# Transposes of attention operands: from TensorE and VectorE copies to DMA transposes on the SP queue

## Chip, cores, metric

One core of a Trainium2 chip. The metric is the device time of one execution in microseconds, all runs in the fast state unless said.

## The reference, cut

Attention over keys and values that are averaged in groups of 8, for 8 batches, 8 heads, 576 rows, head size 64; then a mixture of 4 two-layer networks on the 4608 x 512 result.

```python
k_p = k.reshape(B, H, Sp, pool, D).mean(axis=3)          # Sp = 72
v_p = v.reshape(B, H, Sp, pool, D).mean(axis=3)
scores = scale * np.matmul(q, k_p.transpose(0, 1, 3, 2))
attn = softmax(scores)                                    # exp, sum, division
x = (attn @ v_p) -> (4608, 512)
for e in range(4):
    h = np.maximum(x @ w1[e], 0.0)                        # 512 -> 1024
    out += p[:, e:e + 1] * (h @ w2[e])                    # 1024 -> 512
```

## The kernel before

The matmuls of the networks (`up`, `down`) run in chunks of 512 rows, one for each batch (chunk c takes the first 512 rows of batch c) and a ninth for the 64 remainder rows of each batch. While chunk c runs, the attention of batch c + 1 is cut into pieces that are slipped in between its groups of eight matmuls. A chunk has 32 slots for pieces, one after each `up` or `down` group. Attention needs four kinds of transposes: the keys (`kpT`), the queries (`qT`, `qTr` for the remainder rows), and the attention's result (`xT`, `x_rem`). Before, each is a group of TensorE transposes into PSUM and a copy out of it:

```python
def keys(b, hs):
    kpt_ps = psum_a.tile([P, H, SP], BF16, tag="a", name="kpt_ps")
    for h in range(hs.start, hs.stop):
        nc.tensor.transpose(kpt_ps[:, h, :], state[("kp", b)][:, h], ident[:SP, :SP])
    nc.vector.tensor_copy(out=state[("kpT", b)][:, hs], in_=kpt_ps[:, hs])

def queries(b, pair):                       # 4 pairs of heads a batch
    qt_ps = pool.tile([P, 2, 2, P], BF16, tag=tag, name="qt_ps")
    ...  # 4 transposes of q_sb, then one copy to qT

def flip(x_tok, dst, copy=nc.vector.tensor_copy):   # turn(b, r), rem_turn(i)
    xt_ps = psum_a.tile([P, NPAIR, P], BF16, tag="a", name="xt_ps")
    for kc in range(KC):
        nc.tensor.transpose(xt_ps[:, kc, :], flat[:, kc * P:(kc + 1) * P], ident[:])
    copy(out=dst, in_=xt_ps[:])

# main loop (cut)
per_slot = len(pieces) / (SLOTS - 2 - late)         # late = 16 in chunk 0, else 0
for i in range(NR):
    up(c, e, ...)
    slot()                                          # pops the pieces that are due
    down(*steps[s - 1], i)
    slot()
```

The softmax here doesn't subtract the row's maximum and nothing guards it: scores larger than these inputs give would overflow.

Of the kernel before, what the change touches and what calls it, by code (L numbers as in the profile page):

```python
# [12 lines left out]
BF16 = mybir.dt.bfloat16  # L13
# [4 lines left out]
def kernel(  # L18
# [10 lines left out]
    nc = tc.nc  # L29

    B, H, S, D = q.shape
    E, DM, F = moe_w1.shape
    P = nc.NUM_PARTITIONS
    NPAIR = H // 2
    POOL = 8
    SP = S // POOL
    NT = 512
    NR = NT // P
    REM = S - NT
    KC = DM // P  # L40
# [6 lines left out]
    const = ctx.enter_context(tc.tile_pool(name="const", bufs=1))  # L47
# [14 lines left out]
    w2_bf = wpool.tile([P, E, FCH, DM], BF16, name="w2_bf")  # L62
    x_rem = const.tile([P, NPAIR, NT], BF16, name="x_rem")
    ident = const.tile([P, P], BF16, name="ident")
    vps = [const.tile([SP, H, D + 1], BF16, name=f"vp{i}") for i in range(3)]

    raws = {}
# [33 lines left out]
    def load_k(b):  # L101
        load_kv(b, k, "kraw")
# [49 lines left out]
    def fold_keys(b, hs):  # L152
        raw = raws[("kraw", b)]
        fold(raw, hs)
        if hs.start == 0:
            state[("kp", b)] = apool.tile([SP, H, 2, D], BF16, name="kp")

        for dup in range(2):
            nc.vector.tensor_add(out=state[("kp", b)][:, hs, dup, :], in0=raw[:, hs, 0, :],  # L159
                                 in1=raw[:, hs, 1, :])  # L160

    def keys(b, hs):
        if hs.start == 0:
            state[("kpT", b)] = apool.tile([P, H, SP], BF16, name="kpT")
        kpt_ps = psum_a.tile([P, H, SP], BF16, tag="a", name="kpt_ps")
        for h in range(hs.start, hs.stop):
            nc.tensor.transpose(kpt_ps[:, h, :], state[("kp", b)][:, h], ident[:SP, :SP])  # L167
        nc.vector.tensor_copy(out=state[("kpT", b)][:, hs], in_=kpt_ps[:, hs])

    def fold_values(b, hs):  # L170
        raw = raws[("vraw", b)]
# [5 lines left out]
    def queries(b, pair):  # L177
        q_sb = raws[("q", b)]
        if pair == 0:
            state[("qT", b)] = apool.tile([P, H, 2, P], BF16, name="qT")  # L180
        pool, tag = (psum_o, "o_ps") if b == 0 else (psum_a, "a")
        qt_ps = pool.tile([P, 2, 2, P], BF16, tag=tag, name="qt_ps")
        for hh in range(2):
            for rr in range(2):
                nc.tensor.transpose(  # L185
                    qt_ps[:, hh, rr, :], q_sb[:, 2 * pair + hh, 2 * rr:2 * rr + 2, :], ident[:]
                )
        copy = nc.scalar.copy if b == 0 and pair % 2 else nc.vector.tensor_copy
        copy(out=state[("qT", b)][:, 2 * pair:2 * pair + 2], in_=qt_ps[:])  # L189

    def scores(b, pair):
        kpT, qT = state[("kpT", b)], state[("qT", b)]
        if pair == 0:
            state[("expT", b)] = apool.tile([SP, H, 2, 2, P], BF16, name="expT")
        expT = state[("expT", b)]
        both = [psum_a.tile([P, 2, 2, P], F32, tag="a", name="sc_ps") for _ in range(2)]
        for hh in range(2):
            h = 2 * pair + hh
            for r2 in range(2):
                lo = r2 * D  # L200
                nc.tensor.matmul(  # L201
                    both[r2][0:SP, hh], lhsT=kpT[lo:lo + D, h, :], rhs=qT[lo:lo + D, h]
                )
        for r2 in range(2):
            nc.scalar.activation(  # L205
                out=expT[:, 2 * pair:2 * pair + 2, :, r2, :], in_=both[r2][0:SP],
                func=ACT.Exp, scale=EXP_SCALE,
            )
# [19 lines left out]
            )  # L228
        divide(c_ps, state[("x", b, r)], half)

    def flip(x_tok, dst, copy=nc.vector.tensor_copy):
        xt_ps = psum_a.tile([P, NPAIR, P], BF16, tag="a", name="xt_ps")
        flat = x_tok[:].rearrange("p a h d -> p (a h d)")
        for kc in range(KC):
            nc.tensor.transpose(xt_ps[:, kc, :], flat[:, kc * P:(kc + 1) * P], ident[:])  # L235
        copy(out=dst, in_=xt_ps[:])  # L236

    def turn(b, r):
        if r == 0:
            state[("xT", b)] = xpool.tile([P, KC, NT], BF16, name="xT")  # L240
        flip(state.pop(("x", b, r)), state[("xT", b)][:, :, r * P:(r + 1) * P],
             nc.scalar.copy if b == 0 else nc.vector.tensor_copy)



    def rem_queries(i):
        q_rem = q_rems.pop(i)
        qt_ps = psum_a.tile([P, NPAIR, P], BF16, tag="a", name="qtr_ps")
        for pair in range(NPAIR):
            nc.tensor.transpose(  # L250
                qt_ps[:, pair, :], q_rem[:, 2 * pair:2 * pair + 2, :], ident[:]
            )
        qTr = apool.tile([P, NPAIR, 2, REM], BF16, name="qTr")
        nc.vector.tensor_copy(
            out=qTr[:].rearrange("p a b t -> p (a b t)"),
            in_=qt_ps[:].rearrange("p a t -> p (a t)"),
        )
        state[("qTr", i)] = qTr

    def rem_scores(i):  # L260
        qTr = state.pop(("qTr", i))
        both = [psum_a.tile([P, 2, NPAIR, REM], F32, tag="a", name="scr_ps") for _ in range(2)]
        for bb in range(2):
            kpT = state[("kpT", 2 * i + bb)]
            for pair in range(NPAIR):
                for hh in range(2):
                    lo = hh * D
                    nc.tensor.matmul(  # L268
                        both[hh][0:SP, bb, pair, :], lhsT=kpT[lo:lo + D, 2 * pair + hh, :],
                        rhs=qTr[lo:lo + D, pair, bb, :],  # L270
                    )
        expTr = apool.tile([SP, 2, 2, NPAIR, REM], BF16, name="expTr")
        for hh in range(2):
            nc.scalar.activation(out=expTr[:, hh], in_=both[hh][0:SP],
                                 func=ACT.Exp, scale=EXP_SCALE)
        state[("expTr", i)] = expTr
# [14 lines left out]
        state[("xr", i)] = x_tok  # L291

    def rem_turn(i):
        flip(state.pop(("xr", i)), x_rem[:, :, i * P:(i + 1) * P])

    def attention_first():

# [18 lines left out]
    def attention(b):  # L316

        every = slice(0, H)
        more = b + 1 < B
        pieces = []  # L320
        add = pieces.append

        def folded_keys():
            fold_keys(b, every)
            if more:
                load_k(b + 1)

        def folded_values():
            fold_values(b, every)
            if more:  # L330
                load_v(b + 1)

        def queried(pair):
            queries(b, pair)
            if more and pair == NPAIR - 1:
                load_q(b + 1)
                load_q_rem(b + 1)

        add(folded_keys)
        add(lambda: queried(0))  # L340
        add(folded_values)
        add(lambda: keys(b, every))
        for pair in range(1, NPAIR):
            add(lambda pair=pair: queried(pair))
            add(lambda pair=pair: scores(b, pair - 1))
        add(lambda: scores(b, NPAIR - 1))
        for r in range(NR):
            add(lambda r=r: (context(b, r, 0), context(b, r, 1)))
            if r:
                add(lambda r=r: turn(b, r - 1))  # L350
        add(lambda: turn(b, NR - 1))
        return pieces

    def attention_rem(i):
        return [lambda: rem_queries(i), lambda: rem_scores(i), lambda: rem_context(i),
                lambda: rem_turn(i)]



# [47 lines left out]

    for vp in vps:
        nc.vector.memset(vp[:, :, D:D + 1], float(POOL))
    make_identity(nc, ident[:])  # L410
    steps = [(c, e) for c in range(NCH) for e in range(E)]
    SLOTS = E * NR * 2


    ENG = mybir.EngineType
    with tc.manual_schedule(engines={ENG.PE, ENG.DVE, ENG.Activation, ENG.Pool}):
        load_k(0)
        load_q(0)
        load_v(0)
# [27 lines left out]
        for s in range(len(steps) + 1):  # L447
            if s < len(steps):
                c, e = steps[s]
                if e == 0:  # L450
                    while pieces:
                        pieces.popleft()()
                    if c % 2:
                        pieces.extend(attention_rem(c // 2))
                    if c + 1 < B:
                        pieces.extend(attention(c + 1))

                    late = SLOTS // 2 if c == 0 else 0
                    per_slot = len(pieces) / (SLOTS - 2 - late)
                    due = -late * per_slot  # L460
            for i in range(NR):
                if s < len(steps):
                    n = FCH // NR
                    up(c, e, range(i * n, (i + 1) * n))
                slot()
                if s > 0:
                    down(*steps[s - 1], i)
                slot()
# [30 lines left out]
```

## Time and profile before

| | before |
|---|---|
| time, median of 4 | 573.08 us (573.04 to 573.14) |
| span of the profiled run | 571.3 us |
| TensorE busy, granted clock | 96%, 0.998 |
| VectorE, ScalarE busy | 33%, 41% |
| first `up` matmul of chunk 1, of chunk 8 | 81.64 us, 503.4 us |

TensorE is the engine to read: its busy share is near all of the span. The prediction shows those lines (in a page, PE are TensorE's matmuls, PEld its weight loads, DVE is VectorE, ACT ScalarE, POOL GpSimd, SPq the DMA queue that SP fills; PEclk is the granted clock in tenths, DMA the busy share of the DMA engines in tenths). The DMA queues are wanted for a comparison later (packets, MB, share of 16 engines):

```profile
q0 software_dynamic: 31504, 22.63, 27.4%
q1 hardware_dynamic: 5248, 9.44, 4.9%
```

The first queue holds the loads, issued by GpSimd; the second the stores, issued by SP.

### The profile page before, as it was taken

How to read it: one execution, taken by the hardware profiler on the slowest of the kernel's cores; microseconds unless marked ns; L12 is line 12 of the kernel's file. 1: busy time of each engine (PE TensorE's matmuls, PEld its weight loads, DVE VectorE, ACT ScalarE, POOL GpSimd, SP SyncE). 2: the span in 40 equal slices, each digit the busy share in tenths (PEclk: the TensorE clock that was granted, in tenths of full speed). 3: DMA queues.
4: the chain of work that ended last, by engine and by line, in shares of the span. 5: the costliest groups of instructions: out<-in, count | busy, mean ns of one | idle time of the engine just before them, and what ended most of it. 6: DMA issues, size and time to landing. Idle time of an engine off the chain costs nothing.

```text
span 571.3 us, 7394 instructions
## 1 busy us (share of the span) xinstructions
PE 546.0 (96%) x3107; PEld 259.8 (45%) x3168; DVE 189.9 (33%) x397; ACT 235.2 (41%) x403; POOL 37.5 (7%) x52
## 2 busy tenths in 40 slices
PE   2699999999999999999999999999999999999996
PEld 1344454444444444444444444454445444444442
DVE  3504446134613335144414361346124211220122
ACT  2453534543354344533463335433543344334430
POOL 6410100010101001100110000100000000000000
PEclk9999999999999999999999999999999999999999
DMA  8999932530343005400730016301000010010003
GB/s 127 211 210 203 185 33 76 82 41 1 73 84 42 2 37 108 55 0 20 140 41 1 1 69 89 42 1 56 20 0 1 37 38 1 0 38 37 2 0 75
DMA packets 36787, 32.56 MB, mean 57 GB/s; under 512 B 8576, under 2 KB 30080, under 8 KB 36752
## 3 DMA queue, kind: packets, MB, share of 16 engines
q0 software_dynamic: 31504, 22.63, 27.4%
q1 hardware_dynamic: 5248, 9.44, 4.9%
q8 instruction: 25, 0.41, 0.3%
q14 instruction: 10, 0.08, 0.1%
HBM read 45.16 MB, written 9.44 MB: 96 GB/s over the span
## 4 chain that ended last, share of the span: by engine, by line
PE 90%; DMA 6%; DVE 1%; issue 1%; ACT 1%; POOL 0%; POOLq 0%
PE o_ps L381 42%; PE h_ps L371 41%; DMA q_sb<-in_q_dram 5%; PE sc_ps L201 2%; PE c_ps L226 1%; PE xt_ps L235 1%; PE qt_ps L185 1%; DMA kraw<-in_k_dram 1%; PE kpt_ps L167 0%; DVE x_tok L213 0%; ACT expT L205 0%; PE scr_ps L268 0%; PE c_ps L286 0%; PE qtr_ps L250 0%; POOL kraw L78 0%
## 5 line engine op out<-in xcount | busy, mean ns | idle before, releaser
L375 ACT ACTIVATE H_sb<-h_ps 128x512 bf16<-128x512 f32 x288 | 172.0, 597 | 255.4 <-PE h_ps L371 242.7
L381 PE MATMUL o_ps<-w_bf,H_sb 128*128 128x512 bf16 x1127 | 268.8, 379 | 1.7 <-issue 0.5
L371 PE MATMUL h_ps<-xT,w_bf 128*128 128x512 bf16 x991 | 240.8, 382 | 2.7 <-issue 0.7
L371 PEld LDWEIGHTS <-w_bf 128*128 128x128 bf16 x1152 | 109.4, 98 | 126.9 <-issue 7.9
L381 PEld LDWEIGHTS <-H_sb 128*128 128x128 bf16 x1152 | 108.8, 98 | 122.2 <-issue 1.4
L392 DVE SCALAR_TENSOR_TENSOR acc<-o_ps,p_all,acc 128x512 f32<-128x512 f32 x108 | 81.0, 750 | 214.6 <-PE o_ps L381 191.7
L389 ACT ACTIVATE acc<-o_ps,p_all 128x512 f32<-128x512 f32 x36 | 24.8, 688 | 41.3 <-PE o_ps L381 40.1
L205 ACT ACTIVATE expT<-sc_ps 72x512 bf16<-72x512 f32 x64 | 34.3, 587 | 10.3 <-PE sc_ps L201 10.1
L189 DVE COPY qT<-qt_ps 128x512 bf16<-128x512 bf16 x30 | 12.6, 420 | 71.1 <-PE qt_ps L185 71.0
L213 DVE TENSOR_TENSOR x_tok<-c_ps,inv 128x256 bf16<-128x256 f32 x72 | 30.5, 424 | 2.5
L371 PE MATMUL h_ps<-x_rem,w_bf 128*128 128x512 bf16 x125 | 29.9, 379 | 0.1
L212 DVE RECIPROCAL inv<-c_ps 128x4 f32<-128x4 f32 x72 | 12.6, 176 | 25.7 <-PE c_ps L226 24.5
L78 POOL DMA_DIRECT2D kraw<-in_k_dram x9 | 7.5, 837 | 202.9 <-DVE kp L159 202.5
L147 DVE TENSOR_TENSOR kraw<-kraw 72x2048 bf16<-72x2048 bf16 (+1 forms) x9 | 9.9, 1095 | 29.9 <-DMA kraw<-in_k_dram 29.9
L226 PE MATMUL c_ps<-vp,expT 72*128 72x65 bf16 x256 | 14.8, 200 | 3.4 <-DVE vp L173 2.5
L226 PEld LDWEIGHTS <-expT 72*128 72x128 bf16 x256 | 13.2, 102 | 10.7 <-issue 4.4
L236 DVE COPY xT<-xt_ps 128x512 bf16<-128x512 bf16 x28 | 11.7, 420 | 15.6 <-PE xt_ps L235 15.6
L235 PE MATMUL xt_ps<-ident,x_tok 128*128 128x128 bf16 x144 | 14.9, 229 | 0.3 <-DVE x_tok L213 0.3
L201 PE MATMUL sc_ps<-qT,kpT 64*72 64x256 bf16 x128 | 14.5, 298 | 0.7 <-ACT qT L189 0.4
L235 PEld LDWEIGHTS <-x_tok 128*128 128x128 bf16 x144 | 11.1, 101 | 8.1 <-DVE x_tok L213 0.9
L167 PE MATMUL kpt_ps<-ident,kp 72*128 72x72 bf16 x64 | 3.8, 204 | 10.3 <-DVE kp L159 10.3
L185 PEld LDWEIGHTS <-q_sb 128*128 128x128 bf16 x128 | 10.1, 103 | 7.9 <-DMA q_sb<-in_q_dram 0.8
(39 smaller groups left out, 109.8 us busy)
## 6 DMA issues: line engine op xcount, KB each, us to landing
w_bf<-in_moe_w_dram POOLq DMA_DIRECT2D x8, 1024.0 KB, 23.1
out_dram<-acc SPq DMA_DIRECT2D x32, 256.0 KB, 2.3
kraw<-in_k_dram POOLq DMA_DIRECT2D x7, 576.0 KB, 9.1
vraw<-in_v_dram POOLq DMA_DIRECT2D x7, 576.0 KB, 10.0
q_sb<-in_q_dram POOLq DMA_DIRECT2D x7, 512.0 KB, 6.0
out_dram<-acc SPq DMA_DIRECT2D x8, 128.0 KB, 2.4
kraw<-in_k_dram POOLq DMA_DIRECT2D x2, 288.0 KB, 5.5
vraw<-in_v_dram POOLq DMA_DIRECT2D x2, 288.0 KB, 9.9
```

The source lines that it names most:

```text
L185: nc.tensor.transpose(qt_ps[:, hh, rr, :], q_sb[:, 2 * pair + hh, 2 * rr:2 * rr + 2, :], ident[:])
L189: copy(out=state[("qT", b)][:, 2 * pair:2 * pair + 2], in_=qt_ps[:])
L201: nc.tensor.matmul(both[r2][0:SP, hh], lhsT=kpT[lo:lo + D, h, :], rhs=qT[lo:lo + D, h])
L205: nc.scalar.activation(out=expT[:, 2 * pair:2 * pair + 2, :, r2, :], in_=both[r2][0:SP], func=ACT.Exp, scale=EXP_SCALE,)
L213: nc.vector.tensor_tensor(out=x_tok[:, half], in0=c_ps[:, :, 0:D], in1=inv[:].unsqueeze(2).to_broadcast([P, NPAIR, D]), op=ALU.mult,)
L226: nc.tensor.matmul(c_ps[:, i, :], lhsT=expT[:, h, r // 2, r % 2, :], rhs=vp[:, h, :])
L235: nc.tensor.transpose(xt_ps[:, kc, :], flat[:, kc * P:(kc + 1) * P], ident[:])
L371: nc.tensor.matmul(h_ps[:], lhsT=w1_bf[:, e, kc, fc * P:(fc + 1) * P], rhs=xT[:, kc, :], start=(kc == 0), stop=(kc == KC - 1),)
L375: nc.scalar.activation(out=H_sb[:, fc, :], in_=h_ps[:], func=ACT.Relu)
L381: nc.tensor.matmul(o_ps[:], lhsT=H_sb[:, fc, r * P:(r + 1) * P], rhs=w2_bf[:, e, fc, :], start=(fc == 0), stop=(fc == FCH - 1),)
L389: nc.scalar.activation(out=accs[c][:, r, :], in_=o_ps[:], func=ACT.Copy, scale=prob)
L392: nc.vector.scalar_tensor_tensor(out=dst, in0=o_ps[:], scalar=prob, in1=dst, op0=ALU.mult, op1=ALU.add,)
```

## The change

The intent is to take transposes off the bounding engine. From batch 2 on, keys and queries are transposed by DMAs from the SP queue, one for each batch's keys and one for its queries; so are the turns of batches 1 to 7 and everything of the remainder rows. To give these transfers time, the pieces are put in another order, empty pieces are added, four slots at a chunk's end are left free instead of two (not in chunk 0), and the load of the next k moves from the fold of the keys to after the queries' transpose. The core of the diff:

```diff
+    SPT = -(-SP // 16) * 16                                        # 80 rows for 72
+    kps = [const.tile([SPT, H, 2, D], BF16, name=f"kp{i}") for i in range(2)]
     def keys(b, hs):
+        if b > 1:
+            nc.sync.dma_start_transpose(
+                out=state[("kpT", b)][:], in_=kps[b % 2][:].rearrange("j h a d -> j (h a d)")
+            )
+            return
     def queries(b, pair):
+        if b > 1:
+            nc.sync.dma_start_transpose(
+                out=state[("qT", b)][:].rearrange("p h a t -> p (h a) t"),
+                in_=q_sb[:].rearrange("p h r d -> p (h r d)"),
+            )
+            return
     def turn(b, r):
+        if b:
+            nc.sync.dma_start_transpose(out=dst, in_=x_tok)
+            return
... rem_queries and rem_turn likewise
         def folded_keys():
             fold_keys(b, every)
-            if more:
-                load_k(b + 1)
...     queried(): load_q(b + 1), load_q_rem(b + 1), now also load_k(b + 1)
+            add(lambda: (keys(b, every), queried()))
+            add(folded_values)
+            add(lambda: None)
+            for pair in range(NPAIR):
+                add(lambda pair=pair: scores(b, pair))
-        return [lambda: rem_queries(i), lambda: rem_scores(i), lambda: rem_context(i),
-                lambda: rem_turn(i)]
+        return [lambda: rem_queries(i), lambda: None, lambda: rem_scores(i),
+                lambda: rem_context(i), lambda: rem_turn(i)]
-                    per_slot = len(pieces) / (SLOTS - 2 - late)
+                    per_slot = len(pieces) / (SLOTS - (4 if c else 2) - late)
```

More of the change, by code (lines that the diff above doesn't have):

```diff
@@ L154, in fold_keys @@
         fold(raw, hs)
-        if hs.start == 0:
-            state[("kp", b)] = apool.tile([SP, H, 2, D], BF16, name="kp")
         for dup in range(2):
-            nc.vector.tensor_add(out=state[("kp", b)][:, hs, dup, :], in0=raw[:, hs, 0, :],
+            nc.vector.tensor_add(out=kps[b % 2][0:SP, hs, dup, :], in0=raw[:, hs, 0, :],
                                  in1=raw[:, hs, 1, :])
@@ L163, in keys @@
         if hs.start == 0:
-            state[("kpT", b)] = apool.tile([P, H, SP], BF16, name="kpT")
+            state[("kpT", b)] = apool.tile([P, H, SPT], BF16, name="kpT")
+        if b > 1:
[3 more added lines that the diff above has]
+            return
         kpt_ps = psum_a.tile([P, H, SP], BF16, tag="a", name="kpt_ps")
         for h in range(hs.start, hs.stop):
-            nc.tensor.transpose(kpt_ps[:, h, :], state[("kp", b)][:, h], ident[:SP, :SP])
-        nc.vector.tensor_copy(out=state[("kpT", b)][:, hs], in_=kpt_ps[:, hs])
+            nc.tensor.transpose(kpt_ps[:, h, :], kps[b % 2][0:SP, h], ident[:SP, :SP])
+        nc.vector.tensor_copy(out=state[("kpT", b)][:, hs, 0:SP], in_=kpt_ps[:, hs])
     def fold_values(b, hs):
@@ L180, in queries @@
             state[("qT", b)] = apool.tile([P, H, 2, P], BF16, name="qT")
-        pool, tag = (psum_o, "o_ps") if b == 0 else (psum_a, "a")
+        if b > 1:
[4 more added lines that the diff above has]
+            return
+        pool, tag = (psum_a, "a") if b else (psum_o, "o_ps")
         qt_ps = pool.tile([P, 2, 2, P], BF16, tag=tag, name="qt_ps")
@@ L201, in scores @@
                 nc.tensor.matmul(
-                    both[r2][0:SP, hh], lhsT=kpT[lo:lo + D, h, :], rhs=qT[lo:lo + D, h]
+                    both[r2][0:SP, hh], lhsT=kpT[lo:lo + D, h, 0:SP], rhs=qT[lo:lo + D, h]
                 )
@@ L229, in context @@
         divide(c_ps, state[("x", b, r)], half)
-    def flip(x_tok, dst, copy=nc.vector.tensor_copy):
-        xt_ps = psum_a.tile([P, NPAIR, P], BF16, tag="a", name="xt_ps")
-        flat = x_tok[:].rearrange("p a h d -> p (a h d)")
-        for kc in range(KC):
-            nc.tensor.transpose(xt_ps[:, kc, :], flat[:, kc * P:(kc + 1) * P], ident[:])
-        copy(out=dst, in_=xt_ps[:])
     def turn(b, r):
@@ L240, in turn @@
             state[("xT", b)] = xpool.tile([P, KC, NT], BF16, name="xT")
-        flip(state.pop(("x", b, r)), state[("xT", b)][:, :, r * P:(r + 1) * P],
-             nc.scalar.copy if b == 0 else nc.vector.tensor_copy)
-    def rem_queries(i):
-        q_rem = q_rems.pop(i)
-        qt_ps = psum_a.tile([P, NPAIR, P], BF16, tag="a", name="qtr_ps")
-        for pair in range(NPAIR):
-            nc.tensor.transpose(
-                qt_ps[:, pair, :], q_rem[:, 2 * pair:2 * pair + 2, :], ident[:]
-            )
+        x_tok = state.pop(("x", b, r))[:].rearrange("p a h d -> p (a h d)")
+        dst = state[("xT", b)][:, :, r * P:(r + 1) * P]
+        if b:
+            nc.sync.dma_start_transpose(out=dst, in_=x_tok)
+            return
+        xt_ps = psum_a.tile([P, KC, P], BF16, tag="a", name="xt_ps")
+        for kc in range(KC):
+            nc.tensor.transpose(xt_ps[:, kc, :], x_tok[:, kc * P:(kc + 1) * P], ident[:])
+        nc.scalar.copy(out=dst, in_=xt_ps[:])
+    def rem_queries(i):
         qTr = apool.tile([P, NPAIR, 2, REM], BF16, name="qTr")
-        nc.vector.tensor_copy(
-            out=qTr[:].rearrange("p a b t -> p (a b t)"),
-            in_=qt_ps[:].rearrange("p a t -> p (a t)"),
+        nc.sync.dma_start_transpose(
+            out=qTr[:].rearrange("p a b t -> p a (b t)"),
+            in_=q_rems.pop(i)[:].rearrange("p h d -> p (h d)"),
         )
@@ L268, in rem_scores @@
                     nc.tensor.matmul(
-                        both[hh][0:SP, bb, pair, :], lhsT=kpT[lo:lo + D, 2 * pair + hh, :],
+                        both[hh][0:SP, bb, pair, :], lhsT=kpT[lo:lo + D, 2 * pair + hh, 0:SP],
                         rhs=qTr[lo:lo + D, pair, bb, :],
@@ L293, in rem_turn @@
     def rem_turn(i):
-        flip(state.pop(("xr", i)), x_rem[:, :, i * P:(i + 1) * P])
+        nc.sync.dma_start_transpose(
+            out=x_rem[:, :, i * P:(i + 1) * P],
+            in_=state.pop(("xr", i))[:].rearrange("p a h d -> p (a h d)"),
+        )
     def attention_first():
@@ L331, in folded_values, with queried @@
                 load_v(b + 1)
-        def queried(pair):
-            queries(b, pair)
+        by_pe = b <= 1
+        def queried(pair=NPAIR - 1):
+            queries(b, pair if by_pe else 0)
             if more and pair == NPAIR - 1:
@@ L337, in queried @@
                 load_q_rem(b + 1)
+                load_k(b + 1)
         add(folded_keys)
-        add(lambda: queried(0))
-        add(folded_values)
-        add(lambda: keys(b, every))
-        for pair in range(1, NPAIR):
-            add(lambda pair=pair: queried(pair))
-            add(lambda pair=pair: scores(b, pair - 1))
-        add(lambda: scores(b, NPAIR - 1))
+        if by_pe:
+            add(lambda: queried(0))
+            add(folded_values)
+            add(lambda: keys(b, every))
+            for pair in range(1, NPAIR):
+                add(lambda pair=pair: queried(pair))
+                add(lambda pair=pair: scores(b, pair - 1))
+            add(lambda: scores(b, NPAIR - 1))
+        else:
+            add(lambda: (keys(b, every), queried()))
+            add(folded_values)
+            add(lambda: None)
+            for pair in range(NPAIR):
+                add(lambda pair=pair: scores(b, pair))
         for r in range(NR):
             add(lambda r=r: (context(b, r, 0), context(b, r, 1)))
-            if r:
-                add(lambda r=r: turn(b, r - 1))
-        add(lambda: turn(b, NR - 1))
+            add(lambda r=r: turn(b, r))
         return pieces
     def attention_rem(i):
-        return [lambda: rem_queries(i), lambda: rem_scores(i), lambda: rem_context(i),
-                lambda: rem_turn(i)]
+        return [lambda: rem_queries(i), lambda: None, lambda: rem_scores(i),
+                lambda: rem_context(i), lambda: rem_turn(i)]
     hidden = {}
@@ L409 @@
         nc.vector.memset(vp[:, :, D:D + 1], float(POOL))
+    for kp in kps:
+        nc.vector.memset(kp[SP // 32 * 32:SPT], 0.0)
     make_identity(nc, ident[:])
@@ L415 @@
     ENG = mybir.EngineType
-    with tc.manual_schedule(engines={ENG.PE, ENG.DVE, ENG.Activation, ENG.Pool}):
+    with tc.manual_schedule(engines={ENG.PE, ENG.DVE, ENG.Activation, ENG.Pool, ENG.SP}):
         load_k(0)
```

## The prediction

> **What bounds the kernel now.** I read the page top down: busy shares, slices, then the chain that ended last.
>
> ```profile
> span 571.3 us, 7394 instructions
> PE 546.0 (96%) x3107; PEld 259.8 (45%) x3168; DVE 189.9 (33%) x397; ACT 235.2 (41%) x403; POOL 37.5 (7%) x52
> ...
> PEclk9999999999999999999999999999999999999999
> DMA  8999932530343005400730016301000010010003
> ...
> PE 90%; DMA 6%; DVE 1%; issue 1%; ACT 1%; POOL 0%; POOLq 0%
> ```
>
> TensorE is busy 96% of the span at full granted clock, and 90% of the chain runs through it. The DMA 6% is start-up (the first k and q loads and the weights). The other engines have room, and so have the DMA engines after slice 5 (about 71 us). So whatever leaves TensorE's queue shortens the run, one for one, as long as nothing it fed comes late.
>
> Busy time is no measure of what a transpose costs, since matmuls overlap. The groups of instructions list 144 transposes of x_tok with 229 ns each, and 14.9 us for all; start-to-start distances in the timeline of TensorE say less still:
>
> ```profile
> 229.76 0.41 PE L201 MATMUL sc_ps<-qT,kpT 64*72 64x256 bf16 x4
> 230.10 1.90 PE L371 MATMUL h_ps<-xT,w_bf 128*128 128x512 bf16 x8
> 231.84 0.39 PE L185 MATMUL qt_ps<-ident,q_sb 128*128 128x128 bf16 x4
> 232.06 1.89 PE L381 MATMUL o_ps<-w_bf,H_sb 128*128 128x512 bf16 x8
> ...
> 249.69 0.39 PE L235 MATMUL xt_ps<-ident,x_tok 128*128 128x128 bf16 x4
> 249.91 1.89 PE L371 MATMUL h_ps<-xT,w_bf 128*128 128x512 bf16 x7
> ...
> 277.23 0.43 PE L167 MATMUL kpt_ps<-ident,kp 72*128 72x72 bf16 x8
> 277.49 1.89 PE L381 MATMUL o_ps<-w_bf,H_sb 128*128 128x512 bf16 x7
> ```
>
> First column is the start, second the length. (Some rows count 7 for 8, as some matmul records are missing.) The eight-matmul groups follow each other at 1.73 us, with a transpose group between them or not; the groups themselves delay the next one by 0.22 us (four transposes of x_tok or q, so 55 ns each) and 0.26 us (eight of the keys). That is the price to use.
>
> [...] The trace has 219 ns (median) as its length but 55 ns as its share of the queue[...]. [...] The kernel before holds no DMA transpose[...]. The only SP transfer there is the store:
>
> ```profile
> out_dram<-acc SPq DMA_DIRECT2D x32, 256.0 KB, 2.3
> ```
>
> **The change, part by part.**
>
> Removed from TensorE, as groups: queries of batches 2 to 7, 6 x 4 groups x 0.225 us = 5.4; keys of batches 2 to 7, 6 x 0.26 = 1.6; turns of x_tok for batches 1 to 7, 28 x 0.22 = 6.2; queries of the remainder rows, 4 x 0.22 = 0.9; their turns, 4 x 0.22 = 0.9. In all 288 transposes and 15.0 us. Every matmul that stays is the same. That gives a floor of 573.1 - 15.0 = 558.1 us, 2.6% less.
>
> Removed from VectorE: 24 copies of qT, 28 of xT, 8 for the remainder (0.42 us each, 25 us) and 6 of kpT (0.46 us, 2.7 us). It is 33% busy and off the path, so this is worth nothing by itself; x_tok and psum_a come free a little sooner.
>
> Added to SP, in one in-order queue with the 40 stores: 6 transposes of keys (80x1024), 6 of q (128x2048), 28 of x_tok, 4 of q_rem and 4 of the remainder's x_tok (128x512 each). [...]
>
> Now the windows that these have. A slot is one up or down group and what is slipped in, on average some 1.8 us.
>
> Turns, chunks 1 to 7: the last piece now falls in slot 28 of 32, so four groups, about 7 us, follow it. [...] Chunk 0 keeps slot 30, and at 19 pieces in 14 slots the last context and the last turn fall in the same slot. Before, in slot 30 of chunk 0, both its last turns stand at 77.75 us and chunk 1 begins two groups later, at 81.64. After, two context evictions come first (in this trace 76.09 to 77.27, 1.2 us), leaving some 2.2 us. Loads of q, q_rem and k for batch 2, which the change issues together at about this time, share the DMA engines. I charge 1 us, once.
>
> Keys and queries, batches 2 to 7: issued as one piece, scored three pieces later: 5 slots later in even chunks, 4 in odd ones. SP waits for the fold of the keys (1.21 + 0.69 + 0.76 = 2.7 us on VectorE after the piece before). In odd chunks the fold starts 6 slots ahead of the scores, 10.5 us, so 7.7 us are left; in even chunks SP stands behind a store that waits for its accumulation, about 1 us after the piece, and again 7 to 8 us are left. [...] Any stall here comes six times: I charge 1 us in all.
>
> Remainder queries in chunks 1, 3, 5: issued in slot 2, used in slot 4, 3.5 us later, and behind the first store of the last chunk. That store's issue stands at 86.08 in the timeline and the scores at 87.14 with one group and the transposes between; counted from the slot, the store goes out at about +1.0 us and leaves 2.4 us[...]. I charge 0.3 us three times. Chunk 7 has five pieces only and much room.
>
> Sum: 558.1 + 1 + 1 + 1 = 561 us.
>
> **The rivals.**
>
> (a) Nothing waits: all transposes land within their windows and the time is the floor, 558 us. For it: the windows (two empty pieces, four slots at the end) look cut to a measured latency, and the first batches, when DMA is at 9 tenths, stay on TensorE. Against: the remainder's window and chunk 0's last are about as long as my estimate of the transfer.
>
> (b) The wait for a copy becomes a wait for a DMA. If q takes 10 us instead of 5, six score groups stall TensorE by 3 to 4 us each and three remainders by 2: 558 + 6 x 3.5 + 6 = 585, slower than before. For it: [...]nothing in the trace measures it. Against: it would have been visible to whoever set the windows.
>
> (c) SP's order. A transpose behind a store waits for the accumulation that the store waits for; the reverse, a store behind a transpose, is harmless because accumulators have two buffers. Costs at most 1 us at each of ten places, in the estimate above already where it matters.
>
> (d) DMA bandwidth becomes a limit. Against: after 86 us the share is 0 to 7 tenths, and transposes add 48 transfers of 128 to 512 KB, 8.6 MB, to the 32.6 MB moved already. Under 2 us, at chunk 0's end alone.
>
> **Range and chances.** The gain of 15.0 us is firm within 1 us, because it is a count times a measured distance. The loss is not: I put 0 to 2 us at four in ten, 2 to 5 at three, 5 to 12 at two and more at one. So 561, with 557 to 570 for eight in ten. The 2% line is at 573.1 x 0.98 = 561.6 us, right beside the prediction. Faster by over 2%: 0.54. Within: 0.40. Slower needs over 26 us of stalls: 0.06.
>
> **What would show it.** TensorE's transposes should be down by 288, its groups else unchanged, and the chunk length in undisturbed stretches down by the removed groups. Idle time of TensorE ahead of sc_ps and scr_ps, and ahead of the first h_ps of a chunk, put down to DMA qT, qTr or xT, is the loss; I expect some 3 us in all, most of it at about 80 us and in slots 2 to 4 of odd chunks. Issue to landing of xT should be 2 to 3.5 us and of qT 4 to 7. The prediction is wrong if qT takes over 8 us, if waits for xT recur at every chunk, or if big matmuls become longer while transposes run.

The landing times that these windows are held against were the author's estimate: no trace then held a DMA transpose, so they were not shown. Measured with the change (below), a 128x512 transpose lands 2.4 us after its issue, and keys and queries together 5.6 us after the issue of the keys. That SP's queue keeps its order shows in the same trace: the keys of batch 3 are folded at 148.97 us, but their transpose is issued at 150.23, behind a store that waits for its accumulation until 149.78.

## The result, and the profile after

560.47 us, median of 8 runs (559.96 to 564.09), beside 574.48 us for the kernel before in the same rounds and the earlier ones (573.04 to 575.69, 13 runs). The ratio is 0.9768, 95% interval 0.975 to 0.9787: 2.3% faster. Ratios here and below are the mean time of one kernel's fast runs over the mean of the other's fast runs of the same rounds, so not quite the ratio of the quoted medians.

The page of the changed kernel: span, busy shares, granted clock and DMA share by slice, the SP queue, the chain.

```profile
span 558.2 us, 6905 instructions
PE 531.7 (95%) x2824; PEld 244.6 (44%) x2880; DVE 165.3 (30%) x333; ACT 235.9 (42%) x403; POOL 37.3 (7%) x52
PEclk9999999999999999999999999999999999999999
DMA  9999972571292113920670027513000010010003
q1 hardware_dynamic: 41344, 18.29, 13.7%
PE 86%; DMA 10%; issue 1%; POOL 1%; DVE 1%; SPq 0%; ACT 0%; POOLq 0%
```

The weight loads of TensorE went from 3168 to 2880, which is the 288 transposes (the weight loads are complete; some matmul records are missing). TensorE still bounds. (The 10% of the chain that is DMA is mostly the start: 6% are loads of q_sb and 2% of w_bf.) The timeline of TensorE, in the stretch of a score phase where the kernel before has a transpose group between the big groups:

```profile
282.83 0.41 PE L213 MATMUL sc_ps<-qT,kpT 64*72 64x256 bf16 x4
283.17 1.90 PE L396 MATMUL o_ps<-w_bf,H_sb 128*128 128x512 bf16 x8
284.91 1.89 PE L386 MATMUL h_ps<-xT,w_bf 128*128 128x512 bf16 x8
286.73 0.41 PE L213 MATMUL sc_ps<-qT,kpT 64*72 64x256 bf16 x4
```

The big groups are as long as before (1.89 and 1.90 us; from the start of each to what follows it, 1.74 and 1.82 us), and nothing stands between two score groups but them. What TensorE waited for, from the list of waits (total us, times, longest):

```profile
PE qt_ps L197 <- DMA q_sb<-in_q_dram: 1.9, 1, 1.9
PE scr_ps L274 <- DMA qTr<-q_rem: 0.9, 3, 0.3
PE h_ps L386 <- DMA xT<-x_tok: 0.8, 1, 0.8
```

The second and third are waits for the new transposes; there is none for `qT` and none for `xT` after chunk 1 began. The first is a load's, at the start. The new transfers, issue to landing in us:

```profile
xT<-x_tok SPq DMA_TRANSPOSE x28, 2.4
kpT<-kp SPq DMA_TRANSPOSE x6, 2.7
qT<-q_sb SPq DMA_TRANSPOSE x6, 4.4
qTr<-q_rem SPq DMA_TRANSPOSE x4, 2.4
x_rem<-x_tok SPq DMA_TRANSPOSE x4, 2.6
```

And the timeline of one batch, from the end of the key fold to the first scores (start, length, engine):

```profile
100.48 0.76 DVE L160 TENSOR_TENSOR kp<-kraw 72x512 bf16<-72x512 bf16 x2
101.30 1.20 SPq L167 DMA_TRANSPOSE kpT<-kp  x1
102.61 1.93 SPq L188 DMA_TRANSPOSE qT<-q_sb  x1
107.47 0.89 POOL L89 DMA_DIRECT2D q_sb<-in_q_dram  x1 [41.23 <-DMA qT<-q_sb]
108.10 0.41 PE L213 MATMUL sc_ps<-qT,kpT 64*72 64x256 bf16 x4
```

The queries' transpose is issued at 102.61; with the median landing time of 4.4 us it is there at 107.0, and the next load of q_sb, which waits for it, starts at 107.47. The scores follow at 108.10 without a wait. That leaves about 1 us to spare; counted in the same way, it is 1.1 to 1.6 us in all six batches.

**Where the 13.1 us of the span come from.** Removed transposes 15.0. Given back: 0.75 (`xT`, chunk 1) and 0.9 (`qTr`). The start was unlike: TensorE waits for the load of q_sb of batch 1 at about 52 us, 1.87 us here and 0.30 before, and had begun chunk 0 0.39 us earlier, net 1.2 against the change. After the last matmul the stores took 4.6 us, before 5.5: 0.9 for it. 15.0 - 1.65 - 1.2 + 0.9 = 13.1. In chunks 1 to 7, free of what differs at the start and at the end, `up` of chunk 1 to `up` of chunk 8 took 421.8 us before (81.64 to 503.4) and 408.8 after (82.47 to 491.3): 13.0 less, where the count of groups there (15.0 less the four turns of batch 1, 0.9) less the three waits for `qTr` gives 13.2.

### The profile page after: what moved, and what is told of

It reads as the page before. It is cut to its first block, busy times and chain, and to the rows that moved or that the text cites. A ratio compares the mean times of both kernels' runs of the same rounds, so it can differ in the third digit from the quotient of the medians.

```text
span 558.2 us, 6905 instructions
## 1 busy us (share of the span) xinstructions
PE 531.7 (95%) x2824; PEld 244.6 (44%) x2880; DVE 165.3 (30%) x333; ACT 235.9 (42%) x403; POOL 37.3 (7%) x52
## 3 DMA queue, kind: packets, MB, share of 16 engines
q1 hardware_dynamic: 41344, 18.29, 13.7%
## 4 chain that ended last, share of the span: by engine, by line
PE 86%; DMA 10%; issue 1%; POOL 1%; DVE 1%; SPq 0%; ACT 0%; POOLq 0%
PE o_ps L396 42%; PE h_ps L386 41%; DMA q_sb<-in_q_dram 6%; DMA w_bf<-in_moe_w_dram 2%; PE sc_ps L213 2%; DMA qTr<-q_rem 1%; PE c_ps L238 1%; DVE acc L407 1%; DMA xT<-x_tok 0%; POOL kraw L81 0%; PE scr_ps L274 0%; POOL q_sb L89 0%; PE c_ps L292 0%; POOL vraw L81 0%; PE qt_ps L197 0%
## 5 line engine op out<-in xcount | busy, mean ns | idle before, releaser
L386 PEld LDWEIGHTS <-w_bf 128*128 128x128 bf16 x1152 | 110.7, 98 | 133.7 <-issue 6.9
L396 PEld LDWEIGHTS <-H_sb 128*128 128x128 bf16 x1152 | 110.2, 98 | 131.2 <-issue 3.1
L89 POOL DMA_DIRECT2D q_sb<-in_q_dram x9 | 7.8, 867 | 269.4 <-DMA qT<-q_sb 263.3
L238 PE MATMUL c_ps<-vp,expT 72*128 72x65 bf16 x256 | 14.9, 200 | 3.4 <-DVE vp L179 2.5
L238 PEld LDWEIGHTS <-expT 72*128 72x128 bf16 x256 | 13.2, 102 | 10.8 <-issue 4.4
L213 PEld LDWEIGHTS <-kpT 64*72 64x72 bf16 x128 | 5.3, 111 | 13.2 <-issue 13.1
L173 PE MATMUL kpt_ps<-ident,kp 72*128 72x72 bf16 x16 | 1.3, 224 | 9.9 <-DVE kp L160 9.9
L150 DVE TENSOR_TENSOR vraw<-vraw 72x2048 bf16<-72x2048 bf16 (+1 forms) x9 | 9.9, 1096 | 1.2 <-DMA vraw<-in_v_dram 1.2
L81 POOL DMA_DIRECT2D vraw<-in_v_dram x9 | 7.3, 814 | 15.1 <-DVE vp L179 15.1
L280 ACT ACTIVATE expTr<-scr_ps 72x512 bf16<-72x512 f32 x8 | 4.3, 588 | 5.7 <-PE scr_ps L274 5.7
```

Source lines behind the costliest of these rows:

```text
L81: nc.gpsimd.dma_start(out=raw[:, hs], in_=src[b, hs].rearrange("h (j r) d -> j h r d", r=POOL))
L150: nc.vector.tensor_add(out=raw[:, hs, 0:4, :], in0=raw[:, hs, 0:4, :], in1=raw[:, hs, 4:8, :])
L213: nc.tensor.matmul(both[r2][0:SP, hh], lhsT=kpT[lo:lo + D, h, 0:SP], rhs=qT[lo:lo + D, h])
L238: nc.tensor.matmul(c_ps[:, i, :], lhsT=expT[:, h, r // 2, r % 2, :], rhs=vp[:, h, :])
L386: nc.tensor.matmul(h_ps[:], lhsT=w1_bf[:, e, kc, fc * P:(fc + 1) * P], rhs=xT[:, kc, :], start=(kc == 0), stop=(kc == KC - 1),)
L396: nc.tensor.matmul(o_ps[:], lhsT=H_sb[:, fc, r * P:(r + 1) * P], rhs=w2_bf[:, e, fc, :], start=(fc == 0), stop=(fc == FCH - 1),)
```

## Experiments

Theory: the gain is the queue time of the transposes on TensorE, and the DMA transposes cost nothing as long as nobody waits for them. Rivals: VectorE's and PSUM's relief is the gain; the DMA transposes disturb something; the windows do not matter.

**The control (c1).** No edit.

> The changed kernel again, as the control for the next three and to see which of its TensorE waits repeat. All theories: ratio to the kernel before 0.977. If the wait for q_sb of batch 1 at about 52 us (1.87 us in the first trace of the changed kernel, 0.30 us in that of the kernel before) belongs to the change, it is again over 1.5 us; if it is chance of the start-up loads, it differs. The wait for xT at chunk 1 (0.75 us) and the three waits for qTr (0.9 us in all) should repeat.

560.13 us, ratio 0.9745 (0.9724 to 0.9766). The wait for `qTr` was 0.9 us and for `xT` 0.7 us again. The wait for q_sb was 0.50 us. So it varies between traces of one kernel and is no fixed cost of the change. Over all traces with the changed start it goes from none listed (e5) to 2.7 us (e6); the kernel before has 0.3 and its edit of e1 (below) 1.1. Whether the change shifts its mean, two traces of the old start cannot tell.

**Only the DMA side (e1).** The kernel before, each DMA transpose added beside the TensorE transposes, into a tile without a reader:

```diff
+            un_q = unread.tile([P, H * 2, P], BF16, name="un_q")
+            nc.sync.dma_start_transpose(
+                out=un_q[:], in_=q_sb[:].rearrange("p h r d -> p (h r d)")
+            )
... and un_k, un_x, un_r likewise
```

> The kernel before, with the 48 DMA transposes added into tiles that nobody reads. Theory (a transpose on the SP queue costs nothing unless somebody waits for it): within 0.3% of the kernel before, no matmul longer. Rival (the DMA transposes disturb TensorE's operand reads or the loads): slower by 3 us or more, with longer matmul groups or new waits for q_sb, kraw, vraw.

573.84 us, ratio 0.9998 (0.9986 to 1.001). So these 48 DMA transposes, which TensorE does not wait for, are free, and TensorE does not feel them: its `o_ps` and `h_ps` matmuls take 379 and 381 ns in the mean, before 379 and 382. But the trace held something I had not looked for:

```profile
un_q<-q_sb SPq DMA_TRANSPOSE x6, 18.1
un_k<-kp SPq DMA_TRANSPOSE x6, 11.7
```

The same transfers took 4.4 and 2.7 us in the changed kernel. Here the piece order of the kernel before sets them beside the loads of k and v for the next batch. That made e8 and e9 worth running.

**Only the TensorE side (e2).** The changed kernel with 288 identity transposes back at the places of the removed ones, no copy, no reader:

```diff
+    def again(n, rows=P):
+        ps = psum_a.tile([P, n, rows], BF16, tag="a", name="again_ps")
+        for i in range(n):
+            nc.tensor.transpose(ps[:, i, :], ident[:rows, :], ident[:rows, :rows])
```

> The changed kernel, with the 288 TensorE transposes put back as transposes of the identity, without a copy and without a reader. Theory (the gain is TensorE queue time, 0.22 us for four): 15.0 us slower than the changed kernel less what they hide of its waits (up to 1.6 us), so 13.5 to 15 us, ratio to the kernel before 1.000 to 1.003. Rival (the gain is the removed copies and PSUM turns on VectorE): most of the gain stays, ratio near 0.98. Rival (a transpose costs its busy time of some 100 ns): 28 us slower, ratio 1.02.

574.32 us, ratio 1.0001 (0.9987 to 1.0015), 14.2 us above the control. The whole gain is gone, and no more than it. TensorE's queue time explains it all; 55 ns a transpose was the right price, not the 100 ns of the groups' busy time. (The waits for `qTr` are gone in this trace, as the fillers delay the scores. Its profiled run also records a granted clock of 0.50 from about 19 to 28 us, in the start-up, where the other traces above record 1.00. Their matmuls are as slow there all the same: eight `c_ps` matmuls take 0.60 us at 21.22 us in this trace and at 20.63 us in that of the kernel before, and 0.42 us later in the run. So a recorded 1.00 in the first 25 us is not to be trusted, and the record is no reason for a longer run.)

**Only the VectorE side (e3).** The changed kernel with 66 additions of the length of the removed copies:

```diff
+    def busy():
+        nc.vector.tensor_add(out=spare[:], in0=w2_bf[:, 0, 0, :], in1=w2_bf[:, 0, 1, :])
```

> The changed kernel, with 66 additions of 128x512 bf16 (about 0.42 us each, as the removed copies) put back on VectorE where the copies were, nobody reading the result. Theory (VectorE has room): within 0.5 us of the changed kernel, ratio 0.977 to 0.978. Rival (the removed copies are part of the gain): slower by several us, ratio 0.985 or more.

560.41 us, ratio 0.9753 (0.9729 to 0.9777). VectorE was busy 188.7 us instead of 165.4 in the control, and the time did not change. VectorE's relief is worth nothing. PSUM buffers are not in this test, and e2's transposes take them again; but the list of waits of the kernel before has no wait of TensorE for a PSUM buffer, so their relief had nothing to give.

**The parts alone (e4, e5).** First the turns alone by DMA (conditions for keys and queries switched off, the remainder as before):

```diff
-        by_pe = b <= 1
+        by_pe = True
-        if b > 1:                 # in keys and queries
+        if b > NCH:
```

> Only the turns of x_tok (28) go by DMA; keys, queries and the remainder stay on TensorE. Theory: 28 x 0.22 = 6.2 us saved, 0.75 us given back in the wait for xT at chunk 1: 5.4 us, ratio 0.990 to 0.991. If the parts do not add up (a common cause), far from it.

569.48 us, ratio 0.992 (0.9894 to 0.9946): 4.6 us, with an interval of 3.1 to 6.1 that holds the 5.4.

Then keys and queries alone:

```diff
     def turn(b, r):
-        if b:
-            nc.sync.dma_start_transpose(out=dst, in_=x_tok)
-            return
```

> Only keys and queries of batches 2 to 7 go by DMA; turns and the remainder stay on TensorE. Theory: 5.4 + 1.6 = 7.0 us saved and no wait, ratio 0.988. Rival (score groups wait for qT): less, with waits of TensorE for qT.

568.45 us, ratio 0.991 (0.9881 to 0.994): 5.2 us, not 7.0. Here TensorE waits three times for `qT`, 2.0 us in all: in this piece order the window came out too short by up to 0.7 us in three of six batches. With them the sum is right: 7.0 - 2.0 = 5.0. The parts add up within their intervals: 4.6 + 5.2 + 2.0 + 1.8 - 0.9 makes 12.7, where the 1.8 of the remainder, less its waits of 0.9, is computed and was not run alone.

**No window (e6).** The first scores right after the transposes:

```diff
             add(lambda: (keys(b, every), queried()))
+            add(lambda: scores(b, 0))
             add(folded_values)
-            add(lambda: None)
-            for pair in range(NPAIR):
+            for pair in range(1, NPAIR):
                 add(lambda pair=pair: scores(b, pair))
+            add(lambda: None)
```

> The changed kernel, with the first scores of batches 2 to 7 moved to the piece right after the DMA transposes of keys and queries. Keys and queries together land 5.6 us after the first is issued (1.2 us of issue, then 4.4 us), the window shrinks from 7.7 to about 2.5 to 3 us. Theory (the windows hide the transfers): six waits for qT of some 3 us, 15 to 20 us slower than the changed kernel, ratio 1.00 to 1.01, the gain gone. Rival (the transposes are fast enough that the windows do not matter): ratio stays at 0.977.

596.74 us, ratio 1.0401 (1.0375 to 1.0426): 4% slower than before, and 37 us above the changed kernel, twice what I expected. The waits alone are not that:

```profile
PE sc_ps L213 <- DMA qT<-q_sb: 23.5, 6, 4.1
```

The stretch of one such wait and the one after it (us; busy us of PE, PEld, DVE, ACT, POOL; then granted clock, DMA share, GB/s):

```profile
233.50:237.60 4.10, 0.04 (x1) 0.01 (x1) 0.57 (x2) 0.60 (x1) 0.00 (x0) 0.84 0.79 148
237.60:241.00 3.40, 3.31 (x10) 1.25 (x12) 0.00 (x0) 1.08 (x2) 2.97 (x4) 0.50 0.33 26
```

In 3.4 us after the wait TensorE does 10 matmuls at a granted clock of 0.50. The 37 us less 23.5 of waiting leave 13.5, so each wait costs over half of itself again.

**Filling the wait (e10).** To separate the waiting from the clock, 64 identity transposes ahead of those scores:

```diff
-            add(lambda: scores(b, 0))
+            add(lambda: ([again(H) for _ in range(8)], scores(b, 0)))
```

> The run without window, with 64 identity transposes (3.5 us of TensorE) ahead of the first scores of batches 2 to 7, in the time in which TensorE only waited for qT. It does more work. Theory (of the 36 us that the missing window cost, 23.5 are waiting and the rest is the lower granted clock after each wait of 4 us): the clock stays at 1.00 and the run takes some 584 us, 12 us less than without the filling. Rival (the slow matmuls come from the transfers themselves, which still run): no better than 596 us, or worse by up to 21 us.

587.99 us, ratio 1.0251 (1.0224 to 1.0277). With 384 more transposes it is 9 us faster than without (596.74); 12 us less and 584 us were expected. The filling ahead of the scores of the same batch, and the two stretches after it:

```profile
228.93 3.74 PE L225 MATMUL again_ps<-ident 128*128 128x128 bf16 x64
233.00:238.00 5.00, 4.71 (x24) 2.24 (x26) 0.00 (x0) 2.96 (x5) 3.24 (x4) 1.00 0.64 71
237.00:241.00 4.00, 4.00 (x21) 1.53 (x19) 0.00 (x0) 2.63 (x5) 0.00 (x0) 1.00 1.46 185
```

The clock is 1.00, although the DMA engines move 71 and 185 GB/s here and only 26 in the slow stretch above. Transposes alone, 58 ns apart, kept it up. In the profiled run, the fastest of the four (586.7 us), the sum closes: its span of 584.9 is the control's 558.5 plus 6 x 3.5 of filling plus 5.3 us of waits left. So the rest of the cost of a missing window, about a third, is the clock after an idle TensorE, not the transfers.

**Loads beside the transposes (e9).** The load of k back to the fold, for batches 3 to 7:

```diff
         def folded_keys():
             fold_keys(b, every)
+            if more and b > 1:
+                load_k(b + 1)
...
-                load_k(b + 1)
+                if b <= 1:
+                    load_k(b + 1)
```

> The changed kernel, with the load of the next batch's k (batches 3 to 7) back where the kernel before issues it, right after the fold, so that it runs beside the DMA transposes of keys and queries. Theory (what holds a DMA transpose up is a load in flight: qT landed after 18.1 us beside loads in the unread copy, after 4.4 us alone): qT lands 12 to 18 us after issue, a wait of some 8 us five times and slow matmuls after each, 40 to 60 us slower than the changed kernel, ratio 1.04 to 1.09. Rival (the place of the load in the diff is tidying up): ratio 0.977.

582.31 us, ratio 1.0156 (1.0122 to 1.0191): that one line undoes the gain and 9 us more; it costs 22 us against the changed kernel, where 40 to 60 were expected. The median of `qT` is 8.6 us, not 12 to 18 (one load beside it, not several), and the five waits make 16.4 us. They are of unlike length, which shows where the clock gives way. After waits of 3.67, 2.21, 3.78, 2.80 and 3.90 us, in this order:

```profile
111.30:114.70 3.40, 3.37 (x12) 1.12 (x12) 0.00 (x0) 1.67 (x3) 2.42 (x3) 0.61 0.34 32
164.70:168.10 3.40, 3.35 (x18) 1.55 (x20) 0.00 (x0) 2.04 (x4) 2.42 (x3) 1.00 0.54 98
236.60:240.00 3.40, 3.40 (x11) 1.21 (x12) 0.00 (x0) 1.67 (x3) 2.42 (x3) 0.50 0.36 32
291.20:294.60 3.40, 3.33 (x18) 1.56 (x19) 0.00 (x0) 1.95 (x4) 2.42 (x3) 1.00 0.49 93
363.30:366.70 3.40, 3.33 (x15) 1.16 (x16) 0.00 (x0) 1.89 (x4) 2.43 (x3) 0.69 0.30 29
```

After the two short waits the clock is 1.00 and 18 matmuls fit into 3.4 us; after the three long ones 0.61, 0.50 and 0.69, and 12, 11 and 15 fit. The six waits of e6, 3.7 to 4.1 us, belong to the long ones. The length of one wait did not decide alone: in the start-up of e2 the recorded clock fell at about 18.5 us, when the last wait over 1 us lay 7 us back.

**Batch 1 by DMA too (e8).**

```diff
-        by_pe = b <= 1
+        by_pe = b < 1
-        if b > 1:                 # in keys and queries
+        if b > 0:
```

> The changed kernel, with keys and queries of batch 1 by DMA too, while the weight and batch loads hold the DMA engines at 9 tenths. TensorE sheds another 1.2 us. Theory (a DMA transpose among the loads is 2 to 3 times slower: the first xT took 7.9 us against 2.4 us later): qT takes 8 us or more to land in a window of 4 us, 3 to 6 us slower than the changed kernel, ratio 0.983 to 0.987. Rival (the loads do not matter): 1.2 us faster, ratio 0.975.

574.0 us, ratio 1.0003 (0.9992 to 1.0015): the gain is gone by one batch. The direction was right, the size not (14 us above the changed kernel for 3 to 6 expected): `qT` of batch 1 took 18.4 us to land, and SP 10.4 us to issue it.

```profile
72.13 0.64 PE L213 MATMUL sc_ps<-qT,kpT 64*72 64x256 bf16 x4 [14.60 <-DMA qT<-q_sb]
```

One wait of 14.6 us, then a clock of 0.50 until about 78 us. Keeping batch 1 on TensorE, for 1.2 us of its queue, is what the change had to do while the start-up loads run.

**More slack (e7).** One more empty piece before the remainder's scores, and four free slots in chunk 0 too:

```diff
-        return [lambda: rem_queries(i), lambda: None, lambda: rem_scores(i),
+        return [lambda: rem_queries(i), lambda: None, lambda: None, lambda: rem_scores(i),
-                    per_slot = len(pieces) / (SLOTS - (4 if c else 2) - late)
+                    per_slot = len(pieces) / (SLOTS - 4 - late)
```

> The changed kernel, with one more empty piece between the remainder's transpose and its scores, and four free slots at the end of chunk 0 as in the others. Theory (the waits left are these two windows): no wait for qTr (0.9 us) and none for xT at chunk 1 (0.75 us), 1 to 1.6 us faster than the changed kernel, ratio to the kernel before 0.972 to 0.974 where the changed kernel has 0.9745 to 0.977. Rival (denser pieces in chunk 0 wait for one another instead): no gain.

558.7 us, ratio 0.9734 (0.9712 to 0.9757). No wait for `qTr` or `xT` is left in its trace; a wait of 0.7 us for `expT` in the denser chunk 0 is new. The profiled span is 556.9 us, against 558.2 and 558.5 of the changed kernel. The intervals overlap and the two were not timed in the same rounds, so that it is the faster one is likely, not shown.

## Why the prediction was right

It said 561.0 and the measured median is 560.47. Some of that closeness is luck: it started from the 573.1 us of the first four runs, and over 13 runs the kernel before has 574.48. As a saving it said 12.1 us, and the ratio gives 13.3. The 15.0 us were right; the waits given back, 3 us in the prediction, were 1.65.

- **15.0 us off TensorE, by start-to-start distance.** Right: putting 288 transposes back cost 14.2 us, and the parts of the span add up with 15.0. An estimate with the 100 ns of the busy time (14.9 us for 144 transposes) would have given 29.
- **VectorE's copies are worth nothing.** Right: 66 operations put back changed nothing.
- **1 us at chunk 1 for `xT`.** 0.75 measured, the control 0.7.
- **0.3 us three times for `qTr`.** 0.3 us three times.
- **1 us for keys and queries.** None. The landing time of the pair, the author's estimate, was put about 1 us too long and is 5.6 us (1.2 to issue the keys, then 4.4). The issue of q took 1.3 to 2.0 us, that of `xT` 1.2. The landing of `xT` is 2.4; only the first one, beside the start-up loads, took 7.9. That nothing waits is in part luck: the windows were put at 7 to 8 us and are 6.8 us in chunk 1 (101.30 to 108.10) and 7.3 in chunk 2, so two errors of about 1 us cancelled.
- **Rival (b), a wait for a DMA in place of the copy.** It did not come, but the mechanism is real, and the prediction made it too small: it left out that TensorE comes back from waits of 3.7 us and more at a lower clock, 0.50 to 0.69 in the next 3.4 us (e6, e9), and not where the wait was filled (e10). Waits of 2.2 and 2.8 us were harmless in e9 (clock 1.00 after them).
- **Rival (d), DMA bandwidth.** Put at under 2 us and as a matter of bytes (8.6 MB; its own shapes give 8.85, as the trace has). Right as to the changed kernel only because the change takes the load of k out of the way. Not the bytes are the matter (in e1 the same bytes cost nothing, ratio 0.9998): beside loads, a transpose took two to four times as long (`qT` 8.6 us in e9 and 18.4 in e8 for 4.4, the first `xT` 7.9 for 2.4). The prediction read the moved load as a shift of traffic to chunk 0's end; e9 shows it is a condition of the gain.

Why a transpose suffers so beside loads was not settled. The SP queue went from 5248 to 41344 packets for 8.85 MB more, which makes 245 bytes a packet, where the loads' queue has 718. Whether the small packets are the cause was not shown: no run here varied them.

## What to carry to other kernels

Price an instruction on the bounding engine by what its removal lets start earlier, from start to start, not by its busy time (here 55 ns for a transpose, where the busy time says 100). Work moved to DMA was free here where its window was longer than its landing time (6.8 and 7.3 us for 5.6), and not without that window (e6: 23.5 us of waits, 37 us of time); measure the landing time with the loads that run beside it. Where a load can be issued a little later, that can weigh more than the rest of the change (22 us in e9, for a gain of 13). A wait of the bounding TensorE can cost more than its length: here those of 3.7 us and more did (clock 0.50 to 0.69 after them, e6 and e9), and those of 2.8 and 2.2 us did not (1.00, e9).
